# A Fourier-mixing MLP block with TensorE's sequence fixed as written, the first split by halves, the q = 0 copies on another engine, and more buffers

## The chip, the cores and the metric

The kernel runs on one core of a Trainium2 chip. Its time is what one execution takes on the device, in microseconds (us). A core has five engines with a queue each, which wait for each other through semaphores: TensorE (PE in the profile) multiplies matrices, VectorE (DVE), ScalarE (ACT) and GpSimd (POOL) work on elements, SyncE (SP) issues transfers. The tables of the profile also have PEld, TensorE's weight loads.

## The reference

For 8 batches of 4224 tokens by 192 features: a causal convolution with 7 taps per head (softmax of a small weight table), a Fourier transform over tokens and over features of which the real part is kept, a residual sum and normalisation, and a two-layer MLP.

```python
out = np.einsum('hk,bskhg->bshg', w, x_unf)      # w: softmax over 7 taps
X = np.fft.fft(x, axis=1)
X = np.fft.fft(X, axis=2)
mixed = np.real(X).astype(np.float32)
u = x + mixed
mu = np.mean(u, axis=-1, keepdims=True)
var = np.mean((u - mu) ** 2, axis=-1, keepdims=True)
un = (u - mu) / np.sqrt(var + 1e-06)
ch = np.maximum(un @ w_ch1, 0.0) @ w_ch2
return (u + ch).astype(np.float32)
```

## The kernel before

Each batch passes through these stages; nearly every product is made of three 16-bit products (high by high, high by low, low by high), which is why most stages write a high part on ACT and a low part on DVE.

- **Convolution** (L370): pc = band times windows of x, in 6 chunks of 3 units, copied to xa and stored in a scratch sc in DRAM. Before a chunk, squares (L333) sums its squares on ACT for a common scale.
- **load_x, split_x** (L441, L460): four pieces xs are read back from the scratch in another layout (SP), and split into XH (ACT, L472) and XL (DVE, L473), eight splits a batch. XH and XL are one tile each for the whole program.
- **stage_a** (L479): 16 units of 12 matmuls, pa, split into yh (ACT, L498) and yl (DVE, L499). **stage_b** (L504): 8 units of two halves pb, split into V (ACT L524, DVE L525); V has five buffers. For q = 0 a 128x96 copy of each V goes into V0 (POOL, L531).
- **load_res** (L538): four indirect gathers on POOL bring the rows of x that belong to a tile of 512 tokens, xr, in three buffers.
- **prep** (L549), a generator in six pieces: 18 matmuls pq, three moves into u (ACT, L591), u + xr (POOL, L592), mean and variance mv (DVE), sd (ACT), a row of small operations w, nm, t, y (POOL, L611 to L618), the normalised rows un (ACT, L628, four operations, one buffer), their high part hl (ACT, L638) and low part (POOL, L641, two operations).
- **transposes** (L647): hl goes through a transposing transfer on SP into kt.
- **mlp_hidden** (L667): six units ph of five matmuls; each is followed by hh (ACT, L684) and hlo (DVE, L685). ph has two PSUM buffers. **mlp_out** (L689): four units of 18 matmuls po (L699, L702, L705) in two PSUM buffers, and u = po + u (DVE, L711), which is stored. pc, pa, pb and pq share four PSUM buffers.

A batch has nine tiles: eight of 512 tokens (it 0 to 7) and one of 128 (it 8). The main loop goes over 72 steps n, batch by batch; I call it = 0 to 8 of a batch its steps 0 to 8. Step n's program has mlp_hidden of tile n and mlp_out of tile n - 1 in turns, with the last pieces of prep and the transpose of tile n + 2, the first pieces of prep of tile n + 3 and the gathers of tile n + 4 placed between them; spread (L737) lays the units of the next batch's front (convolution, split_x, stage_a, stage_b) evenly beside them. The tables split_at, a_at and b_at say at which step: for batches from 2 on, the splits of a batch fall into steps 0 to 2 of the batch before it, its stage_a into steps 2 to 4, and stage_b 5 to 7 into its own steps 0 and 1.

That is the program. The order in which an engine gets its instructions is decided by the tile framework: its scheduler simulates a timeline and may take instructions of any later unit as soon as it holds them to be ready, on each engine by itself. A unit of the program, such as the 18 matmuls of an mlp_out, may thus be cut into pieces. tc.issue_after holds an instruction behind another one in the schedule (in_turn holds splits and squares behind the last hh).

Ahead of the main loop batch 0 passes through its front alone, together with the conversion of the MLP weights from float64 (from_float64, L223: ten DVE operations for each part, on raw tiles that borrow other tags), and the first pieces of prep for tiles 0 to 2.

## Time and profile before

| | us |
|---|---|
| runs | 1337.45, 1334.99, 1337.24 |
| median | 1337.24 |
| the profiled execution | 1339.74 |
| its span | 1338.0 |
| mean TensorE clock | 0.96 |
| PE busy in 75 to 100 / 175 to 200 | 20.00 / 21.22 of 25 |
| PE busy in 479.6 to 635 / 635 to 790.4 | 148.12 / 148.52 of 155.4 |
| PE busy in 945.8 to 1101.2 / 1101.2 to 1256.6 | 143.15 / 150.52 of 155.4 |
| PE busy in 1256.6 to 1338 | 77.73 of 81.4 |

The profiled execution is one run on the chip; its span lies 1.74 us below that execution's time. All times of single instructions come from it. The profile groups instructions by line, engine and tile; "out<-in" names the tile written and the tiles read. In a list of instructions a row has its start, its duration, engine, line, operation, tiles, shape and count, and in brackets how long the engine had been idle before it and what ended that wait: an instruction of another engine, a transfer (DMA), "issue" where the trace shows nothing that it waited for, "remote" where the releaser has no name. A group's row has count, busy time, mean ns of one, and idle time before it with its releasers. Idle time of an engine that is not the one that bounds a stage costs nothing.

### The profile page before, as it was taken

How to read it: one execution, taken by the hardware profiler on the slowest of the kernel's cores; microseconds unless marked ns; L12 is line 12 of the kernel's file. 1: busy time of each engine (PE TensorE's matmuls, PEld its weight loads, DVE VectorE, ACT ScalarE, POOL GpSimd, SP SyncE). 2: the span in 40 equal slices, each digit the busy share in tenths (PEclk: the TensorE clock that was granted, in tenths of full speed). 3: DMA queues.
4: the chain of work that ended last, by engine and by line, in shares of the span. 5: the costliest groups of instructions: out<-in, count | busy, mean ns of one | idle time of the engine just before them, and what ended most of it. 6: DMA issues, size and time to landing. Idle time of an engine off the chain costs nothing.

```text
span 1338.0 us, 30108 instructions
## 1 busy us (share of the span) xinstructions
PE 1204.8 (90%) x12224; PEld 943.1 (70%) x12224; DVE 745.0 (56%) x1635; ACT 819.0 (61%) x1562; POOL 666.5 (50%) x1052
## 2 busy tenths in 40 slices
PE   4186689998999989998999989999889998999999
PEld 4175458885777767786778857777567876777767
DVE  7763365456545565456644575446654566555443
ACT  4643387558755686557865586556755667545642
POOL 0236535457445664457444574456634576456520
PEclk9588889998999999999999999999899999999999
DMA  8934395556555566456554576555564444223321
GB/s 274 241 90 125 90 246 142 104 132 166 132 124 128 126 149 144 121 129 167 120 139 103 122 178 127 128 125 129 141 137 108 116 96 95 69 63 84 75 63 39
DMA packets 225819, 170.19 MB, mean 127 GB/s; under 512 B 119560, under 2 KB 207440, under 8 KB 225680
## 3 DMA queue, kind: packets, MB, share of 16 engines
q1 hardware_dynamic: 163408, 108.53, 35.4%
q10 hardware_dynamic: 49600, 33.77, 10.0%
q0 software_dynamic: 12672, 25.97, 7.5%
q8 instruction: 95, 1.56, 0.5%
q14 instruction: 44, 0.36, 0.1%
HBM read 83.73 MB, written 58.55 MB: 106 GB/s over the span
## 4 chain that ended last, share of the span: by engine, by line
PE 35%; POOL 24%; issue 17%; ACT 11%; DVE 5%; DMA 4%; another core or an unknown queue 1%; SPq 1%; ACTq 0%; POOLq 0%; DVEq 0%
PE ph L680 12%; POOL xr L544 11%; PE pa L490 5%; ACT un L628 4%; POOL u L592 4%; PE po L699 4%; PE po L705 4%; PE po L702 4%; POOL hl L641 4%; DMA xs<-sc 3%; PE pc L387 3%; DVE XL L473 2%; PE pq L574 2%; ACT hl L638 2%; ACT hh L684 1%
## 5 line engine op out<-in xcount | busy, mean ns | idle before, releaser
L680 PE MATMUL ph<-kt,W 128*128 128x512 f16 (+1 forms) x2160 | 504.0, 367 | 18.5 <-DMA kt<-hl 8.4
L685 DVE SCALAR_TENSOR_TENSOR hlo<-ph,hh 128x512 f16<-128x512 f32 (+1 forms) x400 | 270.8, 679 | 346.5 <-ACT hh L684 342.0
L699 PE MATMUL po<-W,hh 128*128 128x192 f16 x1584 | 387.9, 248 | 45.7 <-ACT hh L684 34.1
L702 PE MATMUL po<-W,hh 128*128 128x192 f16 x1584 | 387.9, 248 | 1.3 <-issue 1.3
L705 PE MATMUL po<-W,hlo 128*128 128x192 f16 x1584 | 384.1, 247 | 1.8 <-issue 1.5
L684 ACT ACTIVATE hh<-ph 128x512 f16<-128x512 f32 (+1 forms) x400 | 236.5, 593 | 199.2 <-PE ph L680 141.3
L544 POOL DMA_INDIRECT xr<-sc,rows_sb x264 | 283.0, 1072 | 134.4 <-issue 60.7
L680 PEld LDWEIGHTS <-W 128*128 128x128 f16 x2160 | 196.4, 99 | 170.7 <-issue 25.7
L641 POOL TENSOR_TENSOR hl<-un,hl 128x512 f16<-128x512 f32 (+1 forms) x144 | 129.4, 920 | 219.0 <-ACT hl L638 210.4
L699 PEld LDWEIGHTS <-hh 128*128 128x128 f16 x1584 | 155.8, 98 | 58.9 <-ACT hh L684 38.6
L592 POOL TENSOR_TENSOR u<-u,xr 128x768 f32<-128x768 f32 (+1 forms) x72 | 121.1, 1682 | 129.9 <-ACT u L591 129.7
L702 PEld LDWEIGHTS <-hh 128*128 128x128 f16 x1584 | 155.8, 98 | 28.7 <-issue 14.1
L705 PEld LDWEIGHTS <-hlo 128*128 128x128 f16 x1584 | 155.6, 98 | 27.5 <-issue 5.8
L628 ACT ACTIVATE un<-u,nm,y 128x192 f32<-128x192 f32 x256 | 120.2, 539 | 53.9 <-POOL nm L618 49.5
L387 PE MATMUL pc<-xt,band 128*120 128x144 f32 x756 | 120.5, 301 | 24.2 <-DMA band<-line_d 15.0
L387 PEld LDWEIGHTS pc<-xt,band 128*120 128x120 f32 x756 | 107.3, 193 | 32.6 <-issue 16.1
L490 PE MATMUL pa<-c_sb,XH 128*128 128x128 f16 x1024 | 103.2, 223 | 22.2 <-ACT XH L472 19.1
L711 DVE SCALAR_TENSOR_TENSOR u<-po,fo,u 128x384 f32<-128x384 f32 (+1 forms) x136 | 81.4, 599 | 62.1 <-PE po L705 46.7
L473 DVE SCALAR_TENSOR_TENSOR XL<-xs,s_x,XH 128x768 f16<-128x768 f32 x64 | 104.2, 1638 | 17.1 <-ACT XH L472 10.3
L499 DVE SCALAR_TENSOR_TENSOR yl<-pa,yh 99x512 f16<-99x512 f32 x128 | 85.3, 682 | 49.1 <-ACT yh L498 45.7
L472 ACT ACTIVATE XH<-xs,s_x 128x768 f16<-128x768 f32 x64 | 106.3, 1694 | 7.9 <-DMA xs<-sc 7.9
L490 PEld LDWEIGHTS <-XH 128*128 128x128 f16 x1024 | 82.6, 99 | 32.6 <-ACT XH L472 19.7
(125 smaller groups left out, 1461.5 us busy)
## 6 DMA issues: line engine op xcount, KB each, us to landing
out_dram<-u SPq DMA_DIRECT2D x64, 384.0 KB
xt<-in_xw_dram SPq DMA_DIRECT2D x42, 576.0 KB
sc<-xa ACTq DMA_DIRECT2D x42, 540.0 KB
xs<-sc SPq DMA_DIRECT2D x96, 192.0 KB
xs<-sc SPq DMA_DIRECT2D x32, 216.0 KB
xr<-sc,rows_sb POOLq DMA_INDIRECT x264
sc<-xa ACTq DMA_DIRECT2D x7, 450.0 KB
xt<-in_xv_dram SPq DMA_DIRECT2D x6, 504.0 KB
```

The lines of the kernel that those rows point to most:

```text
L387: nc.tensor.matmul(pc[:WR, h - h0], band[:, h, :WR], xt[:, :, h * GRP : (h + 1) * GRP], start=True, stop=True,)
L490: nc.tensor.matmul(pa[:, i], x[:, at], F[:, l], start=(n == 0), stop=(n == 2))
L544: nc.gpsimd.indirect_dma_start(bt.xr[it][:, g], None, bt.sc[:S], bass.IndirectOffsetOnAxis(ap=rows_sb[:, col : col + 1], axis=0),)
L592: nc.gpsimd.tensor_tensor(u[:, :ng], u[:, :ng], xr[:, :ng], op=ALU.add)
L628: nc.scalar.activation(un[:, g], u[:, g], AF.Identity, bias=nm[:, g : g + 1], scale=y[:, g : g + 1],)
L641: lower[0] = nc.gpsimd.tensor_tensor(bl[:, :, o : o + n], un[:, :ng, f], hi[:, :, f], op=ALU.subtract).ins
L680: nc.tensor.matmul(ph[:, n], W1[:, w, ht * 128 : (ht + 1) * 128], kt[:, k], start=(i == 0), stop=(i == len(order) - 1),)
L684: anchor[0] = nc.scalar.activation(hh, ph, AF.Relu).ins
L685: nc.vector.scalar_tensor_tensor(hlo, ph, 0.0, hh, op0=ALU.max, op1=ALU.subtract)
L699: nc.tensor.matmul(po[:, g % 2], hh[:, ht, tk], W2[:, ht, 0], start=(ht == 0), stop=False)
L702: nc.tensor.matmul(po[:, g % 2], hh[:, ht, tk], W2[:, ht, 1], start=False, stop=False)
L705: nc.tensor.matmul(po[:, g % 2], hlo[:, ht, tk], W2[:, ht, 0], start=False, stop=(ht == 5),)
```

## The change

Four things change, with the line numbers moving by one or two.

1. In the main loop TensorE's instructions are issued exactly in the program's order; the other engines stay with the scheduler.
2. split_x cuts a piece by halves of j (32 of the 64 columns, all rows of the piece), where it was by halves of its rows. In the first batch the program has the first half of all four pieces ahead of the second halves.
3. The V0 copy moves from GpSimd to ScalarE.
4. xr has four buffers in place of three, un two in place of one. The gathers of tiles 2 and 3 stand with those of tiles 0 and 1 in the program, no longer behind the first hl. To make room, the raw tiles of w2 go into xa's buffers (they were in hlo's), and pieces 2 and 3 of the first batch's xs into hlo's (they were in yh's and yl's).

```diff
+NPC = len(PIECES)
...
-            t = sb.tile([128, HID], F32, tag=("kt", "hl", "un")[i], name=f"cv{i}_{name}", bufs=(3, 2, 1)[i])
+            t = sb.tile([128, HID], F32, tag=("kt", "hl", "un")[i], name=f"cv{i}_{name}", bufs=(3, 2, 2)[i])
...
-    def raw(name, tag):
-        raws[name] = sb.tile([128, HID, 2], I32, tag=tag, name=f"raw_{name}")
+    def raw(name, tag, n=HID):
+        raws[name] = sb.tile([128, n, 2], I32, tag=tag, name=f"raw_{name}")
...
-                raw(f"w2_{i}", "hlo")[:, : 6 * D].rearrange("p (c e) -> p c e", c=3),
+                raw(f"w2_{i}", "xa", 3 * D)[:, : 6 * D].rearrange("p (c e) -> p c e", c=3),
...
-        tag, bufs = (("yh", 1), ("yl", 1))[i - 2] if b == 0 and i > 1 else ("xs", 2)
-        xs = sb.tile([NA, 9, D], F32, tag=tag, name=f"xs_{b}_{i}", bufs=bufs)
+        tag, bufs, n = ("hlo", 2, 8) if b == 0 and i > 1 else ("xs", 2, 9)
+        xs = sb.tile([NA, n, D], F32, tag=tag, name=f"xs_{b}_{i}", bufs=bufs)
...
-        first = PIECES[i][0]
-        b0, b1 = ((first, first + 4), (first + 4, PIECES[i][1]))[half]
-        src = bt.xs[i][:, b0 - first : b1 - first].rearrange("p b (t j) -> p j (b t)", t=ND)
+        b0, b1 = PIECES[i]
+        js = slice(half * NJ // 2, (half + 1) * NJ // 2)
+        src = bt.xs[i][:, : b1 - b0].rearrange("p b (t j) -> p j (b t)", t=ND)[:, js]
...
-                :, :, ND * b0 : ND * b1
+                :, js, ND * b0 : ND * b1
...
-        nc.gpsimd.tensor_copy(
+        nc.scalar.activation(
             bt.V0.rearrange("p l m c -> p (l m) c")[:, :, it * CG : (it + 1) * CG],
             V.rearrange("p l (m q) c -> p (l m) q c", q=NQ)[:, :, 0],
+            AF.Copy,
         )
...
-            bt.xr[it] = sb.tile([128, 4, D], F32, tag="xr", name=f"xr_{b}_{it}", bufs=3)
+            bt.xr[it] = sb.tile([128, 4, D], F32, tag="xr", name=f"xr_{b}_{it}", bufs=4)
...
-        un = sb.tile([128, 4, D], F32, tag="un", name=f"un_{b}_{it}", bufs=1)
+        un = sb.tile([128, 4, D], F32, tag="un", name=f"un_{b}_{it}", bufs=2)
...
-    for i in range(2 * NPC):
-        split_x(first, i)
+    for half in range(2):
+        for i in range(NPC):
+            split_x(first, 2 * i + half)
...
-    for f in gathers(0) + gathers(1):
+    for f in gathers(0) + gathers(1) + gathers(2) + gathers(3):
         f()
...
-    with tc.issue_after(lower[0]):
-        for f in gathers(2) + gathers(3):
-            f()
...
-        spread(merged, fill)
+        with tc.manual_schedule(engines={mybir.EngineType.PE}):
+            spread(merged, fill)
```

Where instructions stand on an engine, before and now. A row has the line, the operation, the tile written, the tiles read, the shape, and "x4" for four alike. The names carry batch and tile (u_2_3 is tile 3 of batch 2), ph the unit as well, and a serial number at the end.

The first place is GpSimd's queue at the start, from hl of tile 1 on. Before:

```order
L641 TENSOR_TENSOR hl_0_1_838<-un_0_1_833,hl_0_1_838 128x4x128
L641 TENSOR_TENSOR hl_0_1_838<-un_0_1_833,hl_0_1_838 128x4x64
L544 DMA xr_0_2_844<-sc_0_126,rows_sb_239 128x192 x4
L544 DMA xr_0_3_849<-sc_0_126,rows_sb_239 128x192 x4
L531 COPY V0_0_692<-V_0_3_1014 128x12x8
L544 DMA xr_0_4_1177<-sc_0_126,rows_sb_239 128x192 x4
L531 COPY V0_0_692<-V_0_4_1046 128x12x8
L531 COPY V0_0_692<-V_0_5_1093 128x12x8
L531 COPY V0_0_692<-V_0_6_1133 128x12x8
L592 TENSOR_TENSOR u_0_2_967<-u_0_2_967,xr_0_2_844 128x768
```

Now, from the gathers of tile 3 on, which follow those of tiles 0 to 2 (left out: the small operations of tiles 0 and 1 up to hl, with the gathers of tile 5 among them):

```order
L546 DMA xr_0_3_663<-sc_0_126,rows_sb_239 128x192 x4
L594 ISA
L594 TENSOR_TENSOR u_0_0_737<-u_0_0_737,xr_0_0_648 128x768
L546 DMA xr_0_4_1179<-sc_0_126,rows_sb_239 128x192 x4
L594 TENSOR_TENSOR u_0_1_796<-u_0_1_796,xr_0_1_653 128x768
...
L643 TENSOR_TENSOR hl_0_1_848<-un_0_1_843,hl_0_1_848 128x4x128
L643 TENSOR_TENSOR hl_0_1_848<-un_0_1_843,hl_0_1_848 128x4x64
L594 TENSOR_TENSOR u_0_2_967<-u_0_2_967,xr_0_2_658 128x768
L546 DMA xr_0_6_1624<-sc_0_126,rows_sb_239 128x192 x4
```

The gathers of tiles 2 and 3 stand ahead of the first u, those of tiles 4 and 5 moved in behind it, and u of tile 2 no longer has twelve gathers and V0 copies ahead of it: it now stands directly behind hl of tile 1.

The second place is GpSimd's queue in steps 0 and 1 of batch 2, from u to nm of a tile. Before:

```order
L592 TENSOR_TENSOR u_2_4_6077<-u_2_4_6077,xr_2_4_5856 128x768
L531 COPY V0_2_4872<-V_2_7_6028 128x12x8
L611 TENSOR_SCALAR w_2_3_5980<-mv_2_3_5944 128x4
L612 TENSOR_SCALAR nm_2_3_5981<-mv_2_3_5944 128x4
L614 TENSOR_TENSOR t_2_3_5979<-y_2_3_5978 128x4
L544 DMA xr_2_7_6584<-sc_2_1490,rows_sb_239 128x192 x4
L615 TENSOR_TENSOR t_2_3_5979<-t_2_3_5979,w_2_3_5980 128x4
L611 TENSOR_SCALAR w_2_4_6232<-mv_2_4_6140 128x4
L612 TENSOR_SCALAR nm_2_4_6233<-mv_2_4_6140 128x4
L614 TENSOR_TENSOR t_2_4_6231<-y_2_4_6230 128x4
L616 TENSOR_SCALAR t_2_3_5979<-t_2_3_5979 128x4
```

Now:

```order
L594 TENSOR_TENSOR u_2_3_5955<-u_2_3_5955,xr_2_3_5667 128x768
L546 DMA xr_2_7_6649<-sc_2_1495,rows_sb_239 128x192 x4
L613 TENSOR_SCALAR w_2_3_6036<-mv_2_3_6000 128x4
L614 TENSOR_SCALAR nm_2_3_6037<-mv_2_3_6000 128x4
L616 TENSOR_TENSOR t_2_3_6035<-y_2_3_6034 128x4
L617 TENSOR_TENSOR t_2_3_6035<-t_2_3_6035,w_2_3_6036 128x4
L618 TENSOR_SCALAR t_2_3_6035<-t_2_3_6035 128x4
L619 TENSOR_TENSOR y_2_3_6034<-y_2_3_6034,t_2_3_6035 128x4
L620 TENSOR_TENSOR nm_2_3_6037<-nm_2_3_6037,y_2_3_6034 128x4
```

Before, two tiles run through each other, with gathers in the middle of tile 3's small operations and its nm further down; now one tile runs from u through four gathers to its nm, and the next one follows.

The third place is TensorE's queue in step 0 of batch 2, between the ph units 2 and 3. Before:

```order
L516 MATMUL pb_2_7_0_6029<-c16_sb_240,yh_2_3997 128x102
L699 LDWEIGHTS hh_2_0_5784
L699 MATMUL po_2_0_0_6009<-W2_377,hh_2_0_5784 128x192
L702 LDWEIGHTS hh_2_0_5784
L702 MATMUL po_2_0_0_6009<-W2_377,hh_2_0_5784 128x192
L516 LDWEIGHTS yl_2_3998
L516 MATMUL pb_2_7_0_6029<-c16_sb_240,yl_2_3998 128x102
L699 LDWEIGHTS hh_2_0_5784
L699 MATMUL po_2_0_2_6145<-W2_377,hh_2_0_5784 128x192
L680 LDWEIGHTS W1_371
L680 MATMUL ph_2_0_3_5935<-kt_2_0_5447,W1_371 128x512
```

Now there is nothing between these two units: ph units 2 to 5 of step 0 and unit 0 of step 1 follow each other, and only then comes po of tile 0, in one piece:

```order
L682 LDWEIGHTS W1_371
L682 MATMUL ph_2_1_0_6055<-kt_2_1_5762,W1_371 128x512
L701 LDWEIGHTS hh_2_0_5840
L701 MATMUL po_2_0_0_6068<-W2_377,hh_2_0_5840 128x192
L704 LDWEIGHTS hh_2_0_5840
L704 MATMUL po_2_0_0_6068<-W2_377,hh_2_0_5840 128x192
L707 LDWEIGHTS hlo_2_0_5841
L707 MATMUL po_2_0_0_6068<-W2_377,hlo_2_0_5841 128x192
```

Before, po of two PSUM buffers and pb of stage_b are cut into pieces of one to six matmuls that lie between the ph units; now each unit is whole, and none lies between these five.

More of the change, by code (lines that the diff above doesn't have):

```diff
@@ L733 @@
     NT = NJ // JT
-    NPC = len(PIECES)
     NIT = NPAIR + 1
```

## The prediction

> **What bounds the kernel now.** I read the page's busy times and chain first, then busy time in stretches, then the gaps on the engine that is nearest to full.
>
> ```profile
> PE 1204.8 (90%) x12224; PEld 943.1 (70%) x12224; DVE 745.0 (56%) x1635; ACT 819.0 (61%) x1562; POOL 666.5 (50%) x1052
> PE 35%; POOL 24%; issue 17%; ACT 11%; DVE 5%; DMA 4%; another core or an unknown queue 1%; SPq 1%; ACTq 0%; POOLq 0%; DVEq 0%
> ```
>
> TensorE is busy for 90% of the span, but only 35% of the chain that ended last is its work; POOL has 24% of it. So there are stages in which TensorE is held by others. Windows of the start and of one batch period show where (the period is 155.4 us: the same un of two batches starts at 324.18 and 479.66, in rows further down):
>
> ```profile
> 100.00:125.00 25.00, 14.32 (x148) 10.70 (x146) 7.50 (x16) 9.11 (x19) 16.32 (x21) 0.77 0.55 144
> 125.00:150.00 25.00, 21.28 (x171) 15.96 (x171) 12.27 (x40) 7.98 (x19) 13.68 (x19) 0.83 0.27 73
> 150.00:175.00 25.00, 14.71 (x112) 9.80 (x109) 7.62 (x17) 12.91 (x21) 9.75 (x23) 0.86 0.61 138
> 324.20:479.60 155.40, 148.47 (x1531) 116.55 (x1529) 86.57 (x189) 103.12 (x197) 84.39 (x132) 0.98 0.58 134
> ```
>
> The columns are window, length, busy time of PE, PEld, DVE, ACT and POOL, then the TensorE clock. From 100 to 175 us TensorE works 50.3 of 75 us (14.32 + 21.28 + 14.71): 24.7 us are idle, at a clock near 0.8. A steady batch idles for 6.9 of 155.4 us. The steps of batch 1 (from the first ph of a step to that of the next) show that this loss isn't even:
>
> ```profile
> 290.60:310.80 20.20, 19.00 (x212) 14.73 (x210) 12.74 (x30) 14.36 (x27) 13.92 (x20) 1.00 0.41 107
> 310.80:330.30 19.50, 15.36 (x111) 10.21 (x111) 12.31 (x23) 14.99 (x24) 14.11 (x24) 0.85 0.74 187
> ```
>
> Steps 0 and 1, in which the next batch's x is split (XH, XL), idle for 1.20 + 4.14 = 5.3 us, most of a batch's 6.9, and lose clock. I call them the dip. There are six such dips (the splits for batches 2 to 7).
>
> **Term 1, the start (about -18 us).** Gaps on PE, the rows on ACT and POOL around them, and two windows with short gaps that have no releaser:
>
> ```profile
> 105.01 2.32 PE L680 MATMUL ph<-kt,W 128*128 128x512 f16 x10 [0.30 <-DMA kt<-hl]
> 123.32 0.34 PE L699 MATMUL po<-W,hh 128*128 128x192 f16 x1 [7.15 <-ACT hh L684]
> 166.89 4.33 PE L680 MATMUL ph<-kt,W 128*128 128x512 f16 x10 [8.09 <-DMA kt<-hl]
> ...
> 113.81 0.51 ACT L524 ACTIVATE V<-pb 128x408 f16<-128x408 f32 x1 [5.34 <-remote]
> 122.26 0.51 ACT L524 ACTIVATE V<-pb 128x408 f16<-128x408 f32 x1 [7.95 <-remote]
> ...
> 56.99 1.38 POOL L544 DMA_INDIRECT xr<-sc,rows_sb  x1 [56.56 <-DMA xt<-in_xw_dram]
> 83.64 3.61 POOL L592 TENSOR_TENSOR u<-u,xr 128x768 f32<-128x768 f32 x2 [1.17 <-ACT u L591]
> 104.84 1.08 POOL L544 DMA_INDIRECT xr<-sc,rows_sb  x1
> 123.68 1.81 POOL L592 TENSOR_TENSOR u<-u,xr 128x768 f32<-128x768 f32 x1
> 158.84 0.20 POOL L618 TENSOR_TENSOR nm<-nm,y 128x4 f32<-128x4 f32 x1
> ...
> 136.00:143.00 7.00, 3.28 (x28) 1.98 (x27) 1.40 (x5) 0.73 (x2) 3.79 (x4) 0.80 0.36 99
> 109.00:116.00 7.00, 3.76 (x22) 1.65 (x19) 0.76 (x2) 0.51 (x1) 5.61 (x7) 1.00 0.69 249
> ```
>
> Two things are late. kt of step 2 is late because POOL does 12 gathers and four V0 copies (each of which waits for a V) from 104.84 on, u of step 2 only at 123.68, and its nm at 158.84. In after's order the gathers of steps 2 and 3 stand ahead of u of step 0, the V0 copies are gone from POOL, and u of step 2 follows hl of step 1 directly. For steps 0 and 1 POOL took 21 us from u (83.64) to the first ph (105.01); started near 109, kt of step 2 is there at about 130, long before the roughly 34 us of steps 0 and 1 (19.00 + 15.36 in batch 1) are done. So the 8.09 us go, and I count them whole. The second, the 7.15 us on hh, sit behind two V writes on ACT that wait 5.34 and 7.95 us for something that the trace doesn't name; the program has them in ACT's queue ahead of hh. In after's order the hh units and V writes are laid out anew and POOL's streak beside them is gone, so I count the 7.15 as gone, and with it TensorE's short gaps without a releaser at the same places (7.00 - 3.76 = 3.2 and 7.00 - 3.28 = 3.7). Against it stand the gathers of steps 4 and 5, which after's POOL queue has between u and nm of steps 0 and 1: eight of 1.08 us and shorter, with 0.30 between them, are 10 us. POOL waited for DVE and ACT for about half of its 21 us there, so I take 4 of them as reaching kt of step 0, and so the first ph. -8.1 - 7.15 - 6.9 + 4 = **-18**. Bounds: -4 (only the kt wait goes, and the 4 are paid) to -25 (all idle time goes).
>
> **Term 2, the head of the program (0, from -3 to +3).** The float64 conversion of w2 moves behind the scratch stores, since its raw tile now waits for an xa slot. Beside it:
>
> ```profile
> 50.21 1.66 DVE L473 SCALAR_TENSOR_TENSOR XL<-xs,s_x,XH 128x768 f16<-128x768 f32 x1 [6.85 <-DMA xs<-sc]
> 70.93 7.69 DVE L499 SCALAR_TENSOR_TENSOR yl<-pa,yh 99x512 f16<-99x512 f32 x12 [0.51 <-ACT yh L498]
> ```
>
> DVE waits 6.85 us for x here, and after that it is nearly full up to the end of stage a. Ten DVE operations for each half of w2 move, and after's order has about five of them left between XL and yl, some 3 us; there the waits for yh (0.51 here, more before it) take part of it. w2's bytes no longer stand ahead of the scratch stores, so x may come a little sooner; and pa can start before the last half of j is split, one XH of 1.65 us earlier. I take nothing, with 3 us either way.
>
> **Term 3, the steady dips (about +0.5 each).** What one dip looks like, that of batch 2 (with the same un of batch 1):
>
> ```profile
> 466.27 1.24 PE L680 MATMUL ph<-kt,W 128*128 128x512 f16 x5 [0.89 <-DVE hlo L685]
> 478.87 0.24 PE L699 MATMUL po<-W,hh 128*128 128x192 f16 x1 [1.71 <-DVE u L711]
> 482.05 0.34 PE L699 MATMUL po<-W,hh 128*128 128x192 f16 x1 [2.28 <-ACT hh L684]
> ...
> 324.18 1.86 ACT L628 ACTIVATE un<-u,nm,y 128x192 f32<-128x192 f32 x4 [3.46 <-POOL nm L618]
> 479.66 1.86 ACT L628 ACTIVATE un<-u,nm,y 128x192 f32<-128x192 f32 x4 [3.46 <-POOL nm L618]
> ...
> 475.34 0.94 POOL L544 DMA_INDIRECT xr<-sc,rows_sb  x1 [0.30 <-issue]
> 482.40:485.90 3.50, 3.50 (x17) 1.73 (x16) 1.01 (x2) 3.50 (x9) 1.95 (x3) 0.63 0.02 5
> ```
>
> ACT waits 3.46 us for nm, which POOL has behind eight gathers; hh stands behind un, and po behind hh (2.28 us). After's POOL order has nm of step 3 before the next gathers are due, so this wait goes. In its place comes the fixed order on TensorE. In before, ph units of step 0 are separated by pieces of po, pb and pq; in after five ph units follow each other (2 to 5 of step 0 and the first of step 1). Two PSUM buffers hold ph, so each waits for the hlo of two units back, and ACT and DVE have splits in between:
>
> ```profile
> L684 ACT ACTIVATE hh<-ph 128x512 f16<-128x512 f32 x384 | 228.6, 597 | 189.2 <-PE ph L680 132.0 <-issue 28.6 <-PE pc L387 15.3
> L685 DVE SCALAR_TENSOR_TENSOR hlo<-ph,hh 128x512 f16<-128x512 f32 x384 | 261.9, 684 | 338.3 <-ACT hh L684 333.9 <-issue 2.4 <-ACT u L591 0.6
> L472 ACT ACTIVATE XH<-xs,s_x 128x768 f16<-128x768 f32 x56 | 90.2, 1645 | 7.9 <-DMA xs<-sc 7.9
> L472 ACT ACTIVATE XH<-xs,s_x 128x960 f16<-128x960 f32 x8 | 16.3, 2037 | 0.0
> L531 POOL COPY V<-V 128x96 f16<-128x96 f16 x64 | 17.9, 281 | 94.6 <-DVE V L525 94.5
> L591 ACT ACTIVATE u<-pq,g 128x128 f32<-128x128 f32 x64 | 28.0, 437 | 0.0
> L610 ACT ACTIVATE sd<-mv,eps 128x4 f32<-128x4 f32 x64 | 19.0, 296 | 57.7 <-DVE mv L599 52.4 <-DVE hlo L685 3.5 <-issue 1.1
> ```
>
> From the end of ph 2 in step 0: hh 0.6, XH 1.7, XL to 4.0, hlo 3 to 4.6, four bn_stats to 5.5, XL to 7.1, hlo 4 to 7.7; only then may the fifth unit of the row start. TensorE has three units in that time, 1.08 us each (ten matmuls took 2.32 us above, five 1.24), 3.2: a loss of 4.5. In step 1 after's ACT queue from the first hh to the next step's adds up to 19.2 us (six hh at 0.5 from start to start, four XH at 1.6, two un at 1.86, and V, hl, u, sq, xa, sd and a V0 copy for 6.1) beside 16.5 us of TensorE work in that stretch (six ph, 72 matmuls of po at a pace of 0.08 us, 24 of pb at 0.05, 18 of pq at 0.06, 8 of pc at 0.25): 2.7 more. That is 7.2 us of loss. Before's two steps lose 5.3 us idle and, at a clock of 0.85 over 19.5 us, 2.9 more: 8.2. Steps 2 to 4 end in ph units side by side too, and have the other V0 copies on ACT, for which I add 0.5 each. So **+0.5** a dip, +3 for six. The split by halves of j leaves each XH and XL at 864 or 768 elements a row, and XH of 128x768 and of 128x960 differ as their sizes do (1645 and 2037 ns, ratio 1.24 against 1.25), so this costs nothing.
>
> The eight V0 copies a batch on ACT are not in the trace. The nearest rows on ACT are 0.30 us (128x4) and 0.44 us (128x128); on POOL it was 0.28. I take 0.3. One lies in step 1's sum above, the rest partly beside TensorE-bound work. With no cover at all they are 8 x 0.44 = 3.5 a batch; if they hide everywhere, 0. Their removal from POOL frees 2.2 us a batch, and the waits for V before them (94.5 us), which made POOL late, but POOL is only half busy. The fourth xr and second un buffer let gathers and un run ahead and cost nothing on any engine.
>
> Bounds for a dip: -4 (of the 2.28, 1.71 and 0.89 us of gaps 2.2 are left, and the clock that they cost, 0.37 x 3.5 = 1.3, is kept) and +4 (both losses above, clock lost as well, and copies uncovered in part).
>
> Of the clock: it was 0.63 from 482.40 on, right after gaps of 1.71 and 2.28 us. The Trainium skill, "TensorE: Matmul & The Clock Gate", section "Part 1: The HAM clock gate", has the clock halve only after an idle window of about 3.4 us. By that rule the short waits at after's ph units would cost no clock, and six dips would come out 6 x 1.3 = 7.8 us lower, near 1314 in the end. The trace disagrees, as gaps below that length did cost clock here, so I don't count on it.
>
> **Sum.** Against the profiled execution (span 1338.0, 1339.74 in all): 1339.74 - 18 + 0 + 3 = 1324.7. The median of the runs, 1337.24, lies 2.5 below that execution, so the forecast is **1322 us**. Terms 2 and 3 with a spread of 1.5 a dip, and term 1 from -10 to -24, give it a range of its own from 1310 to 1334.
>
> **Rivals.**
> - *The fixed order starves TensorE at the splits* (slower). One mechanism: hh stands behind XH in ACT's queue, ph's two buffers fill, and TensorE may no longer take other work in the meantime, as it did in before, where the interleaved po pieces are what keeps step 0 at 19.00 of 20.20 us. With the +4 of each dip: 1339.74 - 18 + 24 = 1345.7, less 2.5: 1343. It turns the total slower above 3 us a dip. For it: the five-unit row is plain in the order. Against: ACT is busy for only 15 of 19.5 us in step 1 of before, so the queue can pack tighter.
> - *The dip goes* (faster). The wait on nm was what mattered, and the fixed queue has slack: 1339.74 - 18 - 24 = 1297.7, so 1295. For it: the 3.46 us wait that ends a dip. Against: step 1's ACT sum of 19.2 us.
> - *The stall at the start comes back* at other instructions, as its releaser has no name (the V write at 122.26 waits in the program for TensorE alone): 1339.74 - 4 + 3 = 1338.7, so 1336. For it: PE shows gaps without a releaser at the same time. Against: the earlier eight gathers in a row, from 56.99 on, stopped nobody. The Trainium skill, "Runtime: NRT & Kernel Launch", section "Instruction fetch mechanics", says that sequential code streams in mostly hidden; by it the stall isn't code loading, and would go with the order. No row here proves that.
>
> **How the numbers follow.** Forecast 0.54, starved 0.18, dip gone 0.14, stall back 0.14. Measurement tells about 0.2% from no change, so faster means below 1334.6 and slower above 1339.9. Faster: 0.51 of the forecast's 0.54, the 0.14 of the third case and 0.04 of the last, 0.69. Slower: 0.15 of the starved case and 0.03 of the last, 0.18. Same: the other 0.13. A range from 1298 to 1343 leaves out about half of the starved case and half of the one without a dip, some 0.16.
>
> **What would show it.** Term 1: the first ph of step 2 (166.89) comes at 142 to 152, and the unnamed waits of the V writes (5.34, 7.95) are gone. Term 3: un's 3.46 us for nm are gone in each dip, and ph waits for hlo there for about 4 us in place of 0.89; a batch period stays within 2 us of 155.4. A period of 158 or more is the first rival, of 152 or less the second. A first ph later than 109 with unnamed waits on ACT is the third. The prediction fails outright if stage a at the start ends later than 82 us (78.6 now, 70.93 + 7.69), or if TensorE's waits move to xr or kt.

## The result and the profile after

The change makes the kernel slower: 1449.6 us as the median of four runs (1446.92 to 1450.78) beside 1337.35 us for the kernel before (1334.99 to 1337.68), a ratio of 1.0838 with an interval of 1.0820 to 1.0856. The profiled execution took 1450.78 us, its span is 1449.0.

The page of the kernel after, busy times and chain by engine, and the two costliest groups that touch the hidden units:

```profile
PE 1238.3 (85%) x12224; PEld 962.9 (66%) x12224; DVE 757.3 (52%) x1635; ACT 835.6 (58%) x1626; POOL 634.0 (44%) x988
PE 39%; ACT 16%; POOL 15%; issue 14%; DVE 9%; DMA 6%; ACTq 0%; SPq 0%; POOLq 0%; DVEq 0%
...
L682 PE MATMUL ph<-kt,W 128*128 128x512 f16 (+1 forms) x2160 | 513.8, 375 | 117.9 <-DVE hlo L687 113.2
L701 PE MATMUL po<-W,hh 128*128 128x192 f16 x1584 | 401.2, 253 | 0.0
```

TensorE is idle for 210.7 us (1449.0 - 1238.3) in place of 133.2 (1338.0 - 1204.8), and the same matmuls are busy for 33.5 us longer, at a mean granted clock of 0.936 in place of 0.96. What it waits for, first after and then before (waiting engine, line and tile, releaser, us in total, times, longest):

```profile
PE ph L682 <- DVE hlo L687: 113.2, 77, 3.2
PE pa L491 <- ACT XH L473: 32.1, 2, 29.0
PE pa L491 <- issue: 11.8, 14, 1.9
```

```profile
PE po L699 <- ACT hh L684: 34.1, 21, 7.1
PE pa L490 <- ACT XH L472: 19.1, 2, 18.5
...
PE ph L680 <- DVE hlo L685: 7.8, 14, 1.1
```

One wait has grown by 105.4 us: ph for hlo, the buffer two units back. The waits of po for hh (34.1) are gone. Where that lies is read from the start of each step (its first hh on ACT, from the list of instructions in order of time), here for batch 2:

| us, step | 0 | 1 | 2 | 3 | 4 | 5 | 6 | 7 | 8 | batch |
|---|---|---|---|---|---|---|---|---|---|---|
| before, first chip | 20.9 | 19.2 | 17.6 | 19.8 | 20.2 | 16.5 | 18.5 | 14.5 | 8.0 | 155.2 |
| after, first chip | 19.9 | 20.0 | 21.2 | 24.0 | 24.1 | 19.0 | 20.0 | 16.8 | 9.4 | 174.4 |
| before, second chip | 20.9 | 19.7 | 17.7 | 18.9 | 19.1 | 16.5 | 18.5 | 14.5 | 8.0 | 153.8 |
| after, third chip | 19.9 | 20.0 | 21.5 | 21.5 | 21.3 | 17.9 | 20.0 | 16.8 | 9.4 | 168.2 |

(The experiments ran on three chips. I take the chip of the first profiles to be that of runs 1 to 4, as the times agree. The kernel before takes nearly the same on the second and third, 1313.9 and 1313.18 us, so the lower two rows are set side by side.) Steps 0 and 1, the dips, take what they took, 39.9 us and 40.1 before. Steps 2 to 4 are 11.8 us longer, steps 5 to 8 are 7.5 us longer. But a step no longer holds the same work. Over steps 0 and 1 of batch 2, before and then after (window, length, busy time of PE, PEld, DVE, ACT, POOL, then the clock):

```profile
447.42:487.56 40.14, 34.76 (x329) 25.12 (x328) 24.82 (x46) 30.81 (x55) 28.70 (x42) 0.96 0.56 145
```

```profile
479.42:519.33 39.91, 33.24 (x289) 23.27 (x286) 23.98 (x44) 30.52 (x55) 21.41 (x35) 0.87 0.54 129
```

The dips hold 40 matmuls fewer, 19 of po and 18 of pq among them, which the fixed order leaves to steps 2 to 8. At the paces that the prediction uses, 0.08 and 0.06 us, that is some 2.6 us of work (an estimate). So the dips lose that much too, although their length doesn't show it, and about 2.6 of the 19.3 us in steps 2 to 8 are work that came from them. Of the 19.1 us that batch 2 takes longer, 12.3 are idle time of TensorE, and 6.9 are the same 1532 matmuls at a lower clock (0.94 in place of 0.99).

Over the run, batch 1 begins 13.7 us later than before (305.7 against 292.0), batches 1 to 4 add 74.1, batches 5 to 7 add 12.5, 7.5 and 3.2: 111.0, the whole difference of the spans.

The end of step 3 and the begin of step 4 in that batch show the mechanism. ACT's list after, then TensorE's rows of the same time (start, duration; in brackets the idle time before the row):

```profile
556.46 0.59 ACT L686 ACTIVATE hh<-ph 128x512 f16<-128x512 f32 x1
556.94 1.17 ACT L344 ACTIVATE sq<-xt 128x1152 bf16<-128x1152 f32 x1
...
558.50 1.85 ACT L630 ACTIVATE un<-u,nm,y 128x192 f32<-128x192 f32 x4
560.25 0.52 ACT L396 ACTIVATE xa<-pc 120x432 f32<-120x432 f32 x1
560.66 0.84 ACT L640 ACTIVATE hl<-un 128x768 f16<-128x768 f32 x1
561.39 0.60 ACT L686 ACTIVATE hh<-ph 128x512 f16<-128x512 f32 x1
...
557.32 1.24 PE L682 MATMUL ph<-kt,W 128*128 128x512 f16 x5
558.40 0.65 PE L388 MATMUL pc<-xt,band 128*120 128x144 f32 x4
558.89 1.24 PE L682 MATMUL ph<-kt,W 128*128 128x512 f16 x5
562.77 1.73 PE L682 MATMUL ph<-kt,W 128*128 128x512 f16 x5 [2.64 <-DVE hlo L687]
```

Between two hh, from 556.94 to 561.39, ACT has squares, un, xa and hl. TensorE fills both ph buffers, and the next row in its fixed order is a third ph. It stands for 2.64 us. In before, the same block stands between the same two hh:

```profile
517.33 0.59 ACT L684 ACTIVATE hh<-ph 128x512 f16<-128x512 f32 x1
517.80 1.17 ACT L343 ACTIVATE sq<-xt 128x1152 bf16<-128x1152 f32 x1
...
522.25 0.60 ACT L684 ACTIVATE hh<-ph 128x512 f16<-128x512 f32 x1
...
518.98 1.24 PE L680 MATMUL ph<-kt,W 128*128 128x512 f16 x5
520.06 0.28 PE L490 MATMUL pa<-c_sb,XH 128*128 128x128 f16 x2
...
520.74 0.24 PE L699 MATMUL po<-W,hh 128*128 128x192 f16 x1
...
522.91 0.26 PE L699 MATMUL po<-W,hh 128*128 128x192 f16 x1 [1.02 <-ACT hh L684]
```

There the scheduler had put pieces of pa and po behind the second ph, and only 1.02 us were lost. (The size of the wait here is in part the chip's: on the first chip ACT also starts late just ahead of these rows, as run 12 shows. On the third chip, without that, the same ph waits 0.96 us and the first ph of the next step 1.63.)

The written order has six hidden units and four output units in turns, h o h o h o h o h h, so that a step ends with two ph and the next begins with one. Step 0 has only one output unit, that of the small tile 8, so there the line is longer; this is the row that the prediction worked out. The block on ACT isn't the same at each border. In batch 2 it is squares, un, xa and hl at the ends of steps 2 to 4 (4.9 to 5.3 us from one hh to the next), and in steps 5 and 6 it is mainly un, with a wait of 2.15 and 1.78 us for nm from GpSimd (4.26 and 4.55 us; 4.50 in step 6 before).

The start, after: two gathers on POOL (the first and the last of 16 in a row), ACT's waits, and TensorE's:

```profile
60.41 3.17 POOL L546 DMA_INDIRECT xr<-sc,rows_sb  x1 [59.98 <-DMA xt<-in_xw_dram]
82.40 0.95 POOL L546 DMA_INDIRECT xr<-sc,rows_sb  x1 [0.30 <-issue]
...
73.30 0.60 ACT L499 ACTIVATE yh<-pa 99x512 f16<-99x512 f32 x1 [2.40 <-remote]
83.26 0.60 ACT L499 ACTIVATE yh<-pa 99x512 f16<-99x512 f32 x1 [8.14 <-remote]
...
76.88 0.27 PE L491 MATMUL pa<-c_sb,XH 128*128 128x128 f16 x1 [1.91 <-issue]
81.85 0.28 PE L491 MATMUL pa<-c_sb,XL 128*128 128x128 f16 x1 [1.12 <-issue]
90.53 3.67 DVE L500 SCALAR_TENSOR_TENSOR yl<-pa,yh 99x512 f16<-99x512 f32 x6
```

The stall without a name is not gone: it now lies in stage a, which ends at 94.2 us (90.53 + 3.67), and the first hh comes at 126.8 in place of 106.3.

### The profile page after: what moved, and what is told of

Its sections match the earlier page's. It is cut to its first block, busy times and chain, and to the rows that moved or that the text cites. A ratio compares the mean times of both kernels' runs of the same rounds, so it can differ in the third digit from the quotient of the medians.

```text
span 1449.0 us, 30090 instructions
## 1 busy us (share of the span) xinstructions
PE 1238.3 (85%) x12224; PEld 962.9 (66%) x12224; DVE 757.3 (52%) x1635; ACT 835.6 (58%) x1626; POOL 634.0 (44%) x988
## 4 chain that ended last, share of the span: by engine, by line
PE 39%; ACT 16%; POOL 15%; issue 14%; DVE 9%; DMA 6%; ACTq 0%; SPq 0%; POOLq 0%; DVEq 0%
PE ph L682 13%; POOL xr L546 8%; PE po L701 5%; ACT un L630 5%; PE po L704 5%; PE po L707 5%; PE pa L491 4%; ACT XH L473 3%; POOL u L594 3%; DVE XL L474 3%; PE pc L388 3%; ACT hh L686 3%; DVE hlo L687 3%; PE pq L576 2%; PE pb L517 2%
## 5 line engine op out<-in xcount | busy, mean ns | idle before, releaser
L682 PE MATMUL ph<-kt,W 128*128 128x512 f16 (+1 forms) x2160 | 513.8, 375 | 117.9 <-DVE hlo L687 113.2
L682 PEld LDWEIGHTS <-W 128*128 128x128 f16 x2160 | 199.8, 100 | 305.2 <-issue 160.5
L701 PE MATMUL po<-W,hh 128*128 128x192 f16 x1584 | 401.2, 253 | 0.0
L707 PE MATMUL po<-W,hlo 128*128 128x192 f16 x1584 | 399.6, 252 | 1.9 <-DVE hlo L687 1.9
L704 PE MATMUL po<-W,hh 128*128 128x192 f16 x1584 | 400.4, 253 | 0.0
L546 POOL DMA_INDIRECT xr<-sc,rows_sb x264 | 277.7, 1052 | 138.6 <-issue 60.4
L701 PEld LDWEIGHTS <-hh 128*128 128x128 f16 x1584 | 160.3, 101 | 19.1 <-issue 5.0
L704 PEld LDWEIGHTS <-hh 128*128 128x128 f16 x1584 | 159.9, 101 | 18.6 <-issue 5.0
L707 PEld LDWEIGHTS <-hlo 128*128 128x128 f16 x1584 | 159.7, 101 | 4.3 <-DVE hlo L687 3.3
L491 PE MATMUL pa<-c_sb,XH 128*128 128x128 f16 x1024 | 107.5, 228 | 43.0 <-ACT XH L473 32.1
L388 PE MATMUL pc<-xt,band 128*120 128x144 f32 x756 | 119.5, 298 | 27.7 <-DMA band<-line_d 15.0
L500 DVE SCALAR_TENSOR_TENSOR yl<-pa,yh 99x512 f16<-99x512 f32 x128 | 86.8, 684 | 101.3 <-ACT yh L499 81.5
L499 ACT ACTIVATE yh<-pa 99x512 f16<-99x512 f32 x128 | 75.9, 598 | 107.2 <-PE pa L491 54.1
L474 DVE SCALAR_TENSOR_TENSOR XL<-xs,s_x,XH 128x768 f16<-128x768 f32 (+1 forms) x64 | 101.9, 1599 | 33.6 <-ACT XH L473 33.4
```

The costliest lines, as they stand in the source:

```text
L388: nc.tensor.matmul(pc[:WR, h - h0], band[:, h, :WR], xt[:, :, h * GRP : (h + 1) * GRP], start=True, stop=True,)
L474: nc.vector.scalar_tensor_tensor(part(XL), src, bt.c, part(XH), op0=ALU.mult, op1=ALU.subtract)
L491: nc.tensor.matmul(pa[:, i], x[:, at], F[:, l], start=(n == 0), stop=(n == 2))
L546: nc.gpsimd.indirect_dma_start(bt.xr[it][:, g], None, bt.sc[:S], bass.IndirectOffsetOnAxis(ap=rows_sb[:, col : col + 1], axis=0),)
L682: nc.tensor.matmul(ph[:, n], W1[:, w, ht * 128 : (ht + 1) * 128], kt[:, k], start=(i == 0), stop=(i == len(order) - 1),)
L701: nc.tensor.matmul(po[:, g % 2], hh[:, ht, tk], W2[:, ht, 0], start=(ht == 0), stop=False)
```

## The experiments

Ratios are to the kernel before, run beside each on the same chip: 1336.51 us on the first chip, 1314.81 and 1313.9 on the second, 1313.18 on the third. Times are compared on one chip, or between the second and third, where the kernel before takes nearly the same.

**1. The fixed order taken out** of the changed kernel (first chip).

```diff
-        with tc.manual_schedule(engines={mybir.EngineType.PE}):
-            spread(merged, fill)
+        spread(merged, fill)
```

> The changed kernel with TensorE's order in the main loop left to the scheduler again; all else as changed. Theory A (the fixed order makes ph wait for hlo at the ends of the steps: ph waited 113 us for hlo after, 7.8 before, and steps 2 to 8 of a batch are 18.8 us longer, while steps 0 and 1 are the same): the period falls from 174.3 to 153-157 us, ph waits under 15 us for hlo, the time is 1340 to 1356, what is left above 1337 being the later start (first hh at 126.8 in place of 106.3). Rival R (the V0 copies on ScalarE and the splits by halves fill ACT, whoever orders TensorE): the period stays above 168 and the time above 1420.

Measured: 1344.74 us, ratio 1.0063 (1.0044 to 1.0082), as theory A has it. ph waits for hlo 18.7 us, a little over the 15 expected; a steady batch takes 157.0 to 157.7.

**2. The fixed order alone,** put into the kernel before (first chip), by the same lines.

> The kernel before with TensorE's fixed order in the main loop as the only edit. Theory A: the period is 171 to 176 us, the start as before (first hh at 106), the time 1425 to 1442. Rival R: the period stays under 160 and the time under 1375.

Measured: 1461.76 us, ratio 1.0936 (1.0916 to 1.0955). ph waits for hlo 88.7 us, a steady batch takes 174.5. That is 20 us beyond theory A's range, with the period inside it. Together with run 1 it settles which part it is: the fixed order alone gives the whole loss, everything else together 0.6%. The fixed order alone also loses 12 us more than the whole change does. Some 5 of them are there when batch 1 begins (310.9 against 305.7), behind one wait in step 1 of batch 0, which takes 47.5 us:

```profile
PE pc L387 <- DMA xt<-in_xw_dram: 24.3, 1, 24.3
```

TensorE's next row there is batch 1's convolution, whose windows xt have not landed, and the order leaves it nothing else to take.

**3. The gathers of tiles 2 and 3 back** behind the low parts of tile 1, in the changed kernel (first chip).

```diff
-    for f in gathers(0) + gathers(1) + gathers(2) + gathers(3):
+    for f in gathers(0) + gathers(1):
...
+    with tc.issue_after(lower[0]):
+        for f in gathers(2) + gathers(3):
+            f()
```

> The changed kernel with the gathers of tiles 2 and 3 back behind the first hl. Theory B (sixteen gathers in a row on POOL, 60 to 83 us, slow the issue of pa on TensorE and of yh on ACT: pa has gaps of 0.4 to 1.9 us without a releaser from 70 to 86 and none behind): stage a ends about 12 us earlier (near 80), the first hh comes at 106 to 114, and the stall moves behind 105 us, where 8 to 12 gathers are in a row again; the time is 1436 to 1450, since the later stall gives part of it back. Rival (the later w2 and x loads or the conversion on DVE delay stage a): stage a still ends after 90 and the first hh comes after 120.

Measured: 1469.1 us (two runs), ratio 1.0992 (1.0958 to 1.1027). Theory B holds for the start: stage a ends at 82.2 us in place of 94.2, and the first hh comes at 113.9 against 126.8. It fails for the time, since step 1 of batch 0 takes 46.6 us, with 22.4 of them for xt as above: SyncE issues that load at 173.00 us, behind a transposing transfer at 167.05, and at 151.81 in the changed kernel. Under the fixed order the early gathers are worth 1.4%, and by another way than I thought: they keep batch 1's loads from being late.

**4. The copies of q = 0 back on GpSimd,** in the changed kernel (first chip).

```diff
-        nc.scalar.activation(
+        nc.gpsimd.tensor_copy(
             bt.V0.rearrange("p l m c -> p (l m) c")[:, :, it * CG : (it + 1) * CG],
             V.rearrange("p l (m q) c -> p (l m) q c", q=NQ)[:, :, 0],
-            AF.Copy,
         )
```

> The changed kernel with the V0 copies back on POOL. Theory A: they cost at most 0.3 us each on ACT in steps 0 and 1, so the period is 172 to 174.5 and the time 1440 to 1452. Rival R: ACT gets room and the time falls below 1430.

Measured: 1438.55 us (two runs), ratio 1.0764 (1.0738 to 1.0789), just under theory A's range; ph waits 106.4 us. The copies cost 11 us under the fixed order, a tenth of the loss.

**5. A third PSUM buffer for ph** in the changed kernel, the order still fixed (second chip).

```diff
-        ph = ps.tile([128, 512], F32, tag="h", name=f"ph_{b}_{it}_{hts[-1]}", bufs=2)
+        ph = ps.tile([128, 512], F32, tag="h", name=f"ph_{b}_{it}_{hts[-1]}", bufs=3)
```

(and bufs=4 to bufs=3 for pc, pa, pb and pq, which share the other tag)

> The changed kernel with three PSUM buffers for ph instead of two (and three instead of four for the buffers that pa, pb, pq and pc share). Theory A: the loss of the fixed order is the ph rows that stand side by side at a step's end (ph_4, ph_5, ph_0 with no po among them); each waits for the hlo two rows back, and with two buffers any 5 us block on ScalarE ahead of hh is seen by TensorE. With a third buffer a row waits for the hlo three rows back, some 2.6 us earlier, so that of the 18.3 us of ph waits per batch at least half goes: ph waits for hlo under 60 us in all, steady batch 174.3 -> 160 to 166, 1365 to 1410 us. Rival B: the two buffers do not matter, because over a whole step ScalarE or VectorE supplies hlo at the slower rate anyway: the waits stay above 100 us, 1440 to 1455 us. The buffer taken from the other pool can cost a little in both (estimated 0 to 2 us per batch, on pa and pb).

Measured: 1340.21 us, ratio 1.019 (1.0174 to 1.0205). That is better than theory A's range. A steady batch takes 156.9 us, and the wait is down from 113.2 (101.3 for the changed kernel on the third chip, run 13):

```profile
PE ph L682 <- DVE hlo L687: 23.3, 21, 2.1
```

**6. An evener written order,** h o h h o h o h h o, still fixed, two ph buffers (second chip).

```diff
-        while hid or out:
-            if hid:
-                main.append(hid.pop(0))
-            if out:
-                main.append(out.pop(0))
+        for kind in "hohhohohho":
+            units = hid if kind == "h" else out
+            if units:
+                main.append(units.pop(0))
+        main += hid + out
```

> The changed kernel with another written order in the main loop, the order still fixed on TensorE: a step's six ph units (h) and four po units (o) go h o h h o h o h h o instead of h o h o h o h o h h. At a step's border there are then h h o h in place of h h h; two pairs of h h stand inside the step. Theory A (three rows in a line at the border are what waits): the waits at unit 0 of a step (2 to 2.8 us in five steps of nine) go to under 0.7 us, steady batch 160 to 166, 1370 to 1410 us. Rival B (any fixed order loses this, since ScalarE's and VectorE's blocks move about and only a free order dodges them): the waits move to the pairs within the step and their sum stays, steady batch 171 to 175, 1430 to 1455 us.

Measured: 1364.18 us, ratio 1.0376 (1.0355 to 1.0396); a steady batch takes 161 to 167 us.

```profile
PE ph L682 <- DVE hlo L687: 67.6, 50, 3.3
```

The first ph of steps 3, 5 and 7, which waits 1.97, 1.68 and 1.86 us on the mean of batches 1 to 5 in the changed kernel on the third chip (run 13), now waits for nothing; but that of step 4 now waits 2.67 (1.20 there), and that of step 6 now 1.61 (0.24 there). So theory A holds in its main point, the line of three, but not cleanly: at two borders the wait grows, as rival B has it.

**7. The free order with the gathers spaced** and the copies on GpSimd, the rest of the change kept (second chip).

```diff
-    for f in gathers(0) + gathers(1) + gathers(2) + gathers(3):
+    for f in gathers(0) + gathers(1):
...
     stage_b(first, 1)
+    with tc.issue_after(v0[0]):
+        for f in gathers(2):
+            f()
...
+    with tc.issue_after(lower[0]):
+        for f in gathers(3):
+            f()
```

(v0[0] is the last copy of q = 0 issued so far, that of unit 1)

> The changed kernel with TensorE's order free, the copies of q = 0 back on GpSimd, and the gathers at the start apart: tiles 0 and 1 first, tile 2 behind the copy of V of unit 1, tile 3 behind the low parts of tile 1. Theory C: what the change costs beside the fixed order (1344.7 against 1336.5 us) is the copies on ScalarE, which it needs for step 1 (22.4 us against 19.2 in a steady batch, 1.7 us a batch in all), and the 16 gathers in a row, which stall TensorE between 70 and 86 us: first hh at 104 to 110 in place of 128.6, the steady batch 155 to 156, 1325 to 1336 us. Rival D: neither counts (batch 1 began at 290.1 in the run with the free order, 1.9 earlier than before, whatever its first hh was; the rest is the halves of j or the buffers): 1341 to 1347 us.

Measured: 1313.88 us, ratio 0.9994 (0.9984 to 1.0004): no change against before. Both expectations were made for the first chip. Over its 1336.5 us theory C's times are ratios of 0.991 to 1.000 and rival D's 1.003 to 1.008, so the ratio fits theory C, at its upper edge. The steady batch is 153.6 us, as in the next run, which has neither the halves of j nor the new buffers, so these are worth nothing there.

**8. Tile 2's gathers early, in the kernel before** (second chip): the first addition of the run above, and gathers(3) alone left at the old place.

> The kernel before with one thing changed: the gathers of tile 2 go out behind the copy of V of unit 1 instead of behind the low parts of tile 1. Theory E: 12 gathers in a row (104.8 to 119.9 us) are what stalls TensorE and ScalarE there; with 8 in that row the short gaps of 109 to 122 us shrink and tile 2 is ready earlier; first ph of step 2 at 150 to 156 in place of 161.6, and the time 1325 to 1333 us. Rival F: what batch 1 begins with (its windows and segments) sets the end of the first batch, so that the gain at step 2 is lost by 292 us: 1334 to 1339 us.

Measured: 1309.23 us, ratio 0.9951 (0.9937 to 0.9964). The first hh of step 2 comes at 149.7 and batch 1 begins at 271.9, against 155.0 and 277.9 in the kernel before on that chip (run 12). Theory E's reason fell all the same: TensorE is busy throughout from 105 to 120 us beside the 8 gathers (5.00 of each 5 us), nearly so beside the 12 of run 7 (4.98, 5.00 and 5.00), and in run 12 beside the 12 of the kernel before.

**9. Run 8 with three ph buffers** and three shared ones (second chip).

> The kernel before with the gathers of tile 2 behind the copy of V of unit 1 (as in the run where that alone gave a ratio of 0.995), and with three PSUM buffers for ph and three for the shared ones instead of two and four; the order on TensorE free. Theory A says that two buffers are short only where ph rows stand in a line with nothing between; a free order breaks the line up (ph waited for hlo 8.3 us in all), so the third buffer is worth little here: ratio 0.990 to 0.997. Rival: the free order too pays for the two buffers in its po rows (21.7 us behind hh, 9.1 behind u): under 0.988. Rival: the shared buffers are the scarcer ones: over 0.998.

Measured: 1291.98 us, ratio 0.9833 (0.9808 to 0.9858), 1.7% under the kernel before. A steady batch takes 151.5 us. The rival's time holds: the free order too pays for two buffers. Its reason holds in part. Between run 8 and this one TensorE's waits of po for hh fell from 21.7 to 10.7 us and those of po for u (9.1) are gone, but po now waits 7.8 us for hlo (0.3), and the waits of pa for XH rose from 18.0 to 27.0. Of the 18.0 us between the two spans 6.2 are idle time of TensorE and 11.8 its busy time, at a clock of 0.976 in place of 0.963.

**10. The fixed order with three buffers, the copies on GpSimd and the gathers spaced** (second chip): the edits of 4, 5 and 7 in the changed kernel.

> The changed kernel, its order on TensorE still fixed, with three PSUM buffers for ph (that alone gave a ratio of 1.019), the copies of q = 0 back on GpSimd, and the gathers at the start apart. Theory A: with the line of three ph rows covered, what is left of the loss is the copies ahead of hh on ScalarE (11 us with two buffers, 3 to 6 expected with three) and the late begin of batch 1 (287 against 272 to 277 us): ratio 1.000 to 1.008, steady batch 154 to 156 on a chip where the kernel before takes 1315 us. Rival B (a fixed order still loses by itself): 1.012 to 1.020.

Measured: 1357.02 us, ratio 1.033 (1.0315 to 1.0344), slower than run 5. Both expectations missed. The steady batch is 156 us, a little better than run 5's; but step 1 of batch 0 takes 46.4 us in place of 27.7, with one wait of TensorE, and SyncE's queue beside it:

```profile
163.82 1.76 PE L388 MATMUL pc<-xt,band 128*120 128x144 f32 x6 [28.77 <-DVE XL L474]
...
149.69 1.45 SPq L652 DMA_TRANSPOSE kt<-hl  x1
151.31 4.22 SPq L457 DMA_DIRECT2D xs<-sc  x8
155.63 0.87 SPq L331 DMA_DIRECT2D xt<-in_xw_dram  x2
...
163.71 1.16 ACT L344 ACTIVATE sq<-xt 128x1152 bf16<-128x1152 f32 x1 [1.70 <-DMA xt<-in_xw_dram]
```

The load of xt is issued at 155.63, behind a transposing transfer that waited for hl. ACT's squares, whose wait the trace puts down to this load, start at 163.71 and the convolution at 163.82, as in runs 2 and 3, whose gathers are late too; DVE's XL, which the trace names, ends at about the same time (163.72).

**11. Run 10 with the even order** (second chip).

> The kernel of the run before this one with the even written order (h o h h o h o h h o) in place of h o h o h o h o h h. If rows side by side still cost something with three buffers, the even order, which has two at most, is faster by 0.3 to 1 per cent than its neighbour; if three buffers cover three rows, the two differ by less than 0.3 per cent.

Measured: 1365.15 us, ratio 1.0386 (1.0369 to 1.0403), 0.5% slower than run 10. ph waits 25.5 us for hlo beside 24.1 in run 10. Both expectations missed, as neither had the even order slower. The waits for hlo fit the second, that three buffers cover a line of three; why the even order loses 0.5% was not tried.

**12. The kernel before, with a profile on the second chip.**

> The kernel before, unchanged, once more with a profile, on the chip of these runs. In the first profile TensorE was busy 2.9 of the 10 us from 110 to 120 us, beside 12 gathers in a row on GpSimd. Theory H: the stall beside the gathers belongs to the chip or the launch, since kernels with 8, 12 and 16 gathers in a row ran without it on the chip where the kernel before took 1315 us: where it takes 1313 to 1318 us here, TensorE is busy over 7 of 10 us beside the 12 gathers; where it takes 1333 to 1340 us, 2 to 4 of 10. Rival I: this row of 12 stalls TensorE on any chip (2 to 4 of 10 us), and the chips differ in the steady batch (155.4 us against 153 to 154).

Measured: 1315.32 us. TensorE in the window from 110 to 120 us, beside the same 12 gathers in a row, first on the first chip, then on the second (window, length, busy time of PE, PEld, DVE, ACT, POOL, then the clock):

```profile
110.00:120.00 10.00, 2.93 (x17) 1.23 (x15) 0.58 (x1) 0.51 (x1) 8.00 (x10) 0.82 0.50 165
```

```profile
110.00:120.00 10.00, 10.00 (x88) 8.09 (x86) 5.83 (x12) 5.41 (x11) 7.99 (x13) 1.00 0.66 200
```

Theory H holds. The chips differ in the steady batch as well, so rival I has a share of the truth: 153.8 against 155.2 us, all of it in steps 3 and 4, where on the first chip ACT starts late (the last matmul of pa, and the yh that reads it):

```profile
513.21 0.22 PE L490 MATMUL pa<-c_sb,XL 128*128 128x128 f16 x1
516.83 0.60 ACT L498 ACTIVATE yh<-pa 99x512 f16<-99x512 f32 x1 [3.65 <-PE po L705]
```

The last matmul of the pa that yh reads ended at 513.43, and ACT was free by then, but yh starts 3.40 us later. The matmul of po that the trace names as the releaser ended just before yh, and yh doesn't read it. On the second chip no wait of ACT reaches 1.5 us in a window over the same two steps of that batch.

**13 to 15. The changed kernel, the same with three ph buffers, and that with the order free, on one chip** (the third). The edits are none, that of run 5, and those of runs 5 and 1.

> The changed kernel, unchanged, beside runs with three ph buffers on one and the same chip; it was timed so far only on the chip where the start stalls beside the gathers. Theory A (the loss is in the steady batch, at the ends of steps, and has nothing to do with the chip): a steady batch of 171 to 175 us, ph waiting for hlo over 95 us in all, and a ratio of 1.07 to 1.10 on either chip. Rival J (a good part of the loss was the chip's stalls, which a fixed order passes on to TensorE): on a chip where the kernel before takes 1313 to 1318 us, a steady batch under 166 us and a ratio under 1.055.

> The changed kernel with three ph buffers (three shared ones in place of four), as run before, now on the same chip as the changed kernel itself. Theory A: a ratio to the kernel before of 1.015 to 1.025, so that the third buffer takes back three quarters of the loss; steady batch 156 to 158 us. Rival J: the changed kernel beside it is within 3 per cent of it.

> The same with three ph buffers, TensorE's order free: all other parts of the change in place. Theory A: the fixed order costs little once a row of ph may run two units ahead: 0.3 to 2 per cent between this and its neighbour, ratio to the kernel before 0.990 to 1.012. Rival B (a fixed order loses by itself whatever the buffers): over 3 per cent between the two.

Measured, in this order: 1403.82 us, ratio 1.0689 (1.0671 to 1.0708), a steady batch of 165.8 to 168.2; 1340.02 us, ratio 1.0203 (1.0184 to 1.0222), a steady batch of 156.5 to 156.9; 1302.63 us, ratio 0.9911 (0.9894 to 0.9928), a steady batch of 152.6. TensorE's wait of ph for hlo, as the group of ph has it in each:

```profile
L682 PE MATMUL ph<-kt,W 128*128 128x512 f16 (+1 forms) x2160 | 507.1, 371 | 101.9 <-DVE hlo L687 101.3
```

```profile
L682 PE MATMUL ph<-kt,W 128*128 128x512 f16 (+1 forms) x2160 | 488.8, 365 | 23.7 <-DVE hlo L687 23.4 <-DMA kt<-hl 0.3
```

```profile
L682 PE MATMUL ph<-kt,W 128*128 128x512 f16 (+1 forms) x2160 | 489.2, 362 | 10.2 <-DVE hlo L687 9.1 <-DMA kt<-hl 1.1
```

Beside the 16 gathers TensorE works through on this chip (x100 matmuls in the 10 us from 70, against x28 on the first):

```profile
70.00:80.00 10.00, 6.20 (x100) 5.54 (x97) 7.64 (x17) 9.64 (x19) 7.81 (x8) 1.00 0.30 80
```

```profile
70.00:80.00 10.00, 3.08 (x28) 1.87 (x27) 2.14 (x8) 2.73 (x7) 7.56 (x9) 0.76 0.29 80
```

Run 13 falls between its two theories. Without the first chip's stalls the loss is 6.9% and not 8.4%: most of it is the fixed order, and the fixed order passes more of the chip's late starts on to TensorE (steps 3 and 4 are 24.0 and 24.1 us on the first chip, 21.5 and 21.3 on the third; in before the two chips differ by 0.9 and 1.0 there). The third buffer takes back 63.8 of 90.6 us (1403.82 - 1340.02, and 1403.82 - 1313.18), 70% of the loss. The fixed order still costs 2.9% with three buffers (1340.02 / 1302.63), between the two expectations; where its 37 us lie is seen in part (12.5 us up to the begin of batch 1, 285.4 against 272.9, and 4 us in each steady batch), and why was not tried.

## Why the prediction was wrong, point by point

- **The step that failed is in term 3:** "Steps 2 to 4 end in ph units side by side too, and have the other V0 copies on ACT, for which I add 0.5 each." They took 11.8 us longer in the batch shown, and steps 5 to 8, to which I gave nothing, 7.5; some 2.6 of this sum is work that moved there from the dips. I had read the two-buffer limit rightly and worked it out for the dips alone, where the splits are. The line of ph stands at nearly every step's end, and there a block on ACT does what XH does in the dip: squares, un, xa and hl at the ends of steps 2 to 4 (4.5 us of work between two hh in the rows above), un and its wait for nm in steps 5 and 6. A third ph buffer takes back 70% of the loss (runs 13 and 14), so the two buffers are the cause of the larger part. The rows for it were at hand: un of 1.86 us and hh of 0.6 were in the text.
- **The wait in the dip was right, its balance was luck.** A loss of 4.5 us in step 0's row of ph was forecast; the waits of its last three units come to 4.56 us on the mean of batches 1 to 5 (4.52 on the third chip), and the first unit of step 1, which the forecast took into the row, waits 0.94 more (0.91 before). un's wait of 3.46 us for nm is gone in the dips, as said; shorter ones stand in steps 5 to 7. That steps 0 and 1 together take 39.9 us, 40.1 before, looks like the forecast, but they do so with 40 matmuls fewer, at a clock of 0.87 in place of 0.96. The sum counted the lost clock for the kernel before (2.9 us) and none for the kernel after.
- **Clock.** The row that I set against the Trainium skill, "TensorE: Matmul & The Clock Gate", section "Part 1: The HAM clock gate", proved the better guide: that section has the clock halve after at least one idle window of about 3.4 us. Here shorter waits cost clock too. In step 0 the five matmuls of a ph still took 1.24 us after a wait of 2.04 us, and 2.29 us after the next wait of 2.10 us, at a granted clock of 0.50:

```profile
490.39 1.24 PE L682 MATMUL ph<-kt,W 128*128 128x512 f16 x5 [2.04 <-DVE hlo L687]
493.73 2.29 PE L682 MATMUL ph<-kt,W 128*128 128x512 f16 x5 [2.10 <-DVE hlo L687]
```

  The mean clock fell from 0.96 to 0.936, and the busy time rose by 33.5 us. No term of the sum had that for the kernel after.
- **Term 1 (-18) failed too,** by the third rival, to which I gave 0.14. I took POOL's row of gathers to be gone from beside TensorE; it had moved to stage a and grown to 16, and the unnamed stall went with it (run 3 takes the 16 apart, and stage a ends 12 us earlier). The first hh came 20.5 us later, batch 1 13.7 later. The other half of the term held: the wait for kt of step 2 is gone after, on both chips. On the first it was 8.09 us, on the second it is longer:

```profile
152.37 1.89 PE L680 MATMUL ph<-kt,W 128*128 128x512 f16 x4 [14.17 <-DMA kt<-hl]
```

  Even so the change wins nothing there: the first hh of step 2 is at 155.0 before (second chip) and 158.1 after (third), because the first hh of all comes at 113.7 against 105.5. Of these 8.2 us stage a has 4.1, as it ends at 82.2 against 78.1, which is term 2's head; the rest lies between stage a and the first hh, where the gathers of tiles 4 and 5 stand that I priced at 4 us. No run separates them.
- **Term 2 (0, from -3 to +3):** some 4 us, by the pair just given, and 3.6 on the first chip in run 3 (stage a ends at 82.2 against 78.6).
- **The rival "starves TensorE at the splits"** had the right mechanism and sign, and the wrong place. It was priced at 4 us in each of six dips; the loss came to 19 us in each steady batch, some 2.6 us of it in the dips. The copies of q = 0, priced at 0.3 to 3.5 us a batch, cost 11 us in all under the fixed order (run 4), 1.4 a batch.
- **Its own tests** would have told it apart: the period of 174.4 us is beyond the 158 named for the first rival, the first ph of step 2 came at 171.4 us and not at 142 to 152, and stage a ended at 94.2 us, beyond the 82 at which the prediction was to fail outright.
- **The range** of 1298 to 1343 had no case in which every step loses, though the written order is the same in every step.

## What to carry to other kernels

In this kernel a fixed order on one engine was about as good as the distance that its buffers let it run ahead. Before fixing one, count, at each place where units of one kind stand side by side and not at the worst place only, the longest block of other work between two releases on the engine that frees the buffer. Where the scheduler had cut units up to fill such places, one more buffer on the short ring was worth more than the order written by hand, and it helped the free order too (ratio 0.9833, from 0.9951). Compare steps by the work in them and not by their length alone. A stall without a releaser must not be counted as gone because the work beside it moves.
